# Turns of keys and outputs placed elsewhere, and a half slot in rounded passes, in a linear-attention and mixture-of-experts kernel

## The chip, the cores and the metric

One core of a Trainium2 chip. The time is that of one execution on the device, in microseconds (us). TensorE multiplies matrices, VectorE, ScalarE and GpSimd work on elements, and SyncE issues most of the DMAs.

## The reference

The first part is a linear attention with a decaying state, for 4 x 8 heads of 48 dimensions and 768 tokens:

```python
for t in range(S):
    state = alpha[:, :, t, :, None] * state + einsum('bhd,bhe->bhde', k[:, :, t], v[:, :, t])
    y[:, :, t] = einsum('bhd,bhde->bhe', q[:, :, t], state)
```

Its output, 3072 tokens of 384 numbers, goes through a mixture of 8 experts. Logits are `x @ w_gate` plus a bias by modality, each token goes to the expert of its largest logit, and the result is the softmax weight of that expert times `relu(x @ w1[e]) @ w2[e]`, with 1024 hidden numbers. Everything is in 32-bit floats.

## The kernel before, in words

**Attention.** A loop runs over steps `s` of 12 chunks (two batches of six chunks; a chunk is 128 tokens of two sequences, 16 heads, in two halves `z`). The steps are pipelined by hand: while VectorE scans the decays of a later chunk (`back`, `forth`) and GpSimd and VectorE scale keys and queries with them, TensorE works on chunk `s - 1`, and the output of chunk `s - 2` goes out. In step `s` TensorE does, in this order: `scores(s - 1, z)`, products of scaled keys and queries for both halves; `keys(s - 1)`, the transposes ("turns") of the scaled keys; `rows(s - 2)`, the turns of the outputs back to one row per token; `logits_turned(s - 2)`, the gate's logits; `from_state(s - 1)`, the products with the state; `add_logits(s - 2)`, from step 7 on, which sums ("folds") the logits over the heads' groups by products with a small table; `states(s - 1)`, the new state; `from_values(s - 1)`, masked scores times values. ScalarE copies each result out of PSUM (`scT` scores, `knat` keys, `xs` rows, `lts` logits, `yt` outputs) and passes over the decays once per chunk as a guard against extreme values (`junk`, `amin`). GpSimd masks the scores (`causal`).

Five PSUM banks `b0` to `b4` are handed out in turn (`next_bank`, line 119): a bank that comes up again must have been read before it is written. Scores take two, one per group of heads; key turns one per half; rows two; logits one; `from_state` two, which hold the outputs until `outputs` copies them at the start of the next step. Small products of the routing take one as well.

**Routing.** The tokens' experts are found in groups while the loop runs, and two early slots of 256 tokens are made up from the first chunks. In step 10 `count_early(0)` counts tokens per expert, and in step 11 `early_places(0)` (line 648) multiplies tables (`OL`, `OHE`) that VectorE makes from that count, to get the tokens of slot 0.

**Experts.** 12 slots of 256 tokens of one expert, then one half slot of 128. A product in full 32-bit precision is carried out as two passes; the slots use rounded operands (`F32R`), where a number is split into a high and a low part and a product takes three rounded passes. `layer1` (line 1197) runs `block` four times: six pairs of products, one of the high weights with high and low inputs side by side (512 columns), and one of the low weights with the high inputs (256 columns). ScalarE copies the low half out (`low`), VectorE adds (`hs`), ScalarE applies the relu and rounds (`hH`), VectorE makes the low part (`hL`), and both split two eighths of the second layer's weights (`w2H`, `w2L`). `layer2` (line 1213) then runs 24 products of 384 columns for each 128 tokens. The splits of the next slot's first-layer weights (`w1H`, `w1L`) stand inside `layer2`. `half` (line 1245) works otherwise: its first layer is in full precision, 24 products of 128 columns on unsplit weights.

**Order.** `Ordered` keeps every engine's instructions in the program's order until `order.clear()` (line 1322); `half(NS0)` comes after that, so that the planner may mix its instructions with those of slot 11. The routing for tokens that don't fit the 13 slots (`tail`) is not executed with these inputs.

Of the kernel before, what the change touches and what calls it, by code (L numbers as in the profile page):

```python
# [21 lines left out]
P = 128  # L22
# [12 lines left out]
T = 256  # L35
# [40 lines left out]
def attention_moe(ctx: ExitStack, tc: tile.TileContext, q, k, v, alpha, at_, kt_, qt_, vt_, mid, wg, wgp_, mb, w1, w2, out):  # L76
# [46 lines left out]
    def bank(*shape):  # L123
        return ps.tile([P, *shape], F32, name=next_bank())
# [241 lines left out]
                vec.tensor_copy(S1, kv)  # L366
            st[s, "S"] = S1

    def from_values(s):
        yk, vt = st[s, "yp"], VT[s % NV]  # L370
        for z in range(2):
            for j in range(NP):
                for x in range(2):
                    g = x ^ z
                    h = DM * z + D * head(z, j, g)
                    pe.matmul(
                        yof(yk, z, x, j),
                        vt[:, h : h + 64],
                        st[s, "s", z][:, g, j],
                        start=new(s, z, x),  # L380
                        stop=(j == NP - 1),
                    )
# [563 lines left out]
    for s in range(PS):  # L946
        if 0 < s and s + 1 < PS:
            load(s + 1, "kqv")
        if 0 <= s - 2:
            outputs(s - 2)  # L950
        late, by = [], vec
        if s == 0:
            warm(14)
            begin(0)
            for z in ZS:
                back(0, z)
                scaled_keys(0, z, pool)
                totals(0, z)
                forth(0, z)
                scaled_queries(0, z, pool if z == Z0 else vec)  # L960
        elif s == 1:
            begin(1)
            scores(0, 0)
            for z in range(2):
                turn_keys(0, z)
                if z == 0:
                    warm(2)
            back(1, Z0)
            scaled_keys(1, Z0, pool)
            scores(0, 1)  # L970
            totals(1, Z0)
            forth(1, Z0)
            scaled_queries(1, Z0, pool)
            back(1, Z1)
            scaled_keys(1, Z1, pool)
            totals(1, Z1)
            forth(1, Z1)
            scaled_queries(1, Z1)
        else:
            if (s - 1, "S") not in st:  # L980
                state(s - 1)
            decayed(s - 1)
            run(s, "state")
            for z in range(2):
                scores(s - 1, z)
            run(s, "masks")
            todo = scans(s)
            if len(todo) > 1:
                late = todo.pop()
            if s >= 4:  # L990
                by = pool
            for f in todo:
                do(f)
            run(s, "counts")
        if 1 < s:
            keys(s - 1)
        if 0 <= s - 2:
            rows(s - 2)
        if 0 <= 2 * (s - 3) < TURNED:
            turn_logits(s - 3)  # L1000
        if 0 <= s - 2:
            logits_turned(s - 2)
        run(s, "small")
        if 0 <= 2 * (s - 3) < TURNED:
            sum_logits(s - 3)
        run(s, "middle")
        do(late[:-1])
        if 0 <= s - 1:
            from_state(s - 1)
        if 0 <= s - 1 and (s - 1) % NC == 0:  # L1010
            states(s - 1)
        if TURNED <= 2 * (s - 2):
            add_logits(s - 2)
        if 0 <= s - 1 and (s - 1) % NC:
            states(s - 1)
        run(s, "sums")
        for f, *x in late[-1:]:
            f(*x, by)
        if 0 <= s - 1:
            from_values(s - 1)  # L1020
        run(s, "end")
        for c in range(s - (s < 5), s + 1 - (s < 4)):
            if 0 <= c < PS:
                guard(c)
        if 0 <= s - 2:
            store(s - 2)
        for c in range(s + 2 + (s > 4), s + 3 + (s > 3)):
            if c < PS:
                load(c, "a")
        if s == 0:  # L1030
            sp.dma_start(wgp, wgp_)
        if s == 1:
            sp.dma_start(mi.rearrange("p t w -> p (t w)"), mid.bitcast(I32))
            sp.dma_start(mbb, mb.unsqueeze(0).broadcast_to([P, NM, E]))
        if s == 2:
            sp.dma_start(xd[MID : MID + 1], of[0:1])
            sp.dma_start(gd[MID : MID + 1], of[0:1, 0:1])
# [135 lines left out]
    XL.append(XB[1][:, :, 1])  # L1173
    ms = {}

    def block(i, w1):
        wH, wL = w1
        hs = mp.tile([P, 2, T], F32, name="hs")
        low = mp.tile([P, 2, T], F32, name="low")
        for z in range(2):  # L1180
            hp = bank(2, T)
            fs = slice(z * P, (z + 1) * P)
            for d in range(ND):
                pe.matmul(hp, wH[:, d, fs], XB[i % 2][:, d], start=(d == 0), stop=False)
                pe.matmul(hp[:, 1], wL[:, d, fs], XH[i % 2][:, d], start=False, stop=(d == ND - 1))
            act.copy(low[:, z], hp[:, 1])
            vec.tensor_tensor(hs[:, z], hp[:, 0], low[:, z], op=ALU.add)
        return hs

    def second_input(hs):  # L1190
        hH = mp.tile([P, 2, T], F32R, name="hH", bufs=5)
        act.activation(hH, hs, AF.Relu)
        hL = mp3.tile([P, 2, T], F32R, name="hL", bufs=5)
        vec.scalar_tensor_tensor(hL, hs, 0.0, hH.bitcast(F32), op0=ALU.max, op1=ALU.subtract)
        return hH, hL

    def layer1(i, w1s):
        W2 = WR[i % 2][1]
        h, w2s = [], []
        for j in range(4):  # L1200
            hs = block(i, w1s[j])
            w2s.append(split("w2", W2[:, 2 * j : 2 * j + 2]))
            h.append(second_input(hs))
        ms[i] = h, w2s

    def scaled_out(i, u, op):
# [3 lines left out]
        if order and u == 0 and i in (NS0 // 2, NS0 - 1):  # L1210
            pool.drain()

    def layer2(i, ahead=()):
        h, w2s = ms[i]
        w1s = []
        for u in range(2):
            us = slice(u * P, (u + 1) * P)
            op = py.tile([P, 512], F32, name=f"y{u}")[:, :DM]
            for f in range(NF):
# [17 lines left out]

    def slot(i, w1s=None):
        layer1(i, w1s or [f() for f in w1_parts(i)])
        if i + 1 < NS and i < NS0:  # L1240
            prep(i + 1)
        refill(i + 2)
        return layer2(i, w1_parts(i + 1) if order and i + 1 < NS0 else ())

    def half(i):

        W1, W2 = WR[i % 2]
        g = gg[i % NX]
        hs, w2s = [], []
        w2s += [split("w2", W2[:, 2 * z : 2 * z + 2]) for z in (0, 1)]  # L1250
        for j in range(2):
            hp = bank(4, P)
            for z in range(4):
                fs = slice((4 * j + z) * P, (4 * j + z + 1) * P)
                for d in range(ND):
                    pe.matmul(hp[:, z], W1[:, d, fs], xf[:, d, :P], start=(d == 0), stop=(d == ND - 1))
            hH = mp.tile([P, 4, P], F32R, name="hH", bufs=5)
            relu = act.activation(hH, hp, AF.Relu)
            hL = mp3.tile([P, 4, P], F32R, name="hL", bufs=5)
            vec.scalar_tensor_tensor(hL, hp, 0.0, hH.bitcast(F32), op0=ALU.max, op1=ALU.subtract)  # L1260
            hs.append((hH, hL))
            if j == 0:
                with tc.issue_after(relu.ins):
                    w2s += [split("w2", W2[:, 2 * z : 2 * z + 2]) for z in (2, 3)]
        op = py.tile([P, 512], F32, name="y0")[:, :DM]
        for f in range(NF):
            (hH, hL), (wH, wL) = hs[f // 4], w2s[f // 2]
            pe.matmul(op, hH[:, f % 4], wH[:, f % 2], start=(f == 0), stop=False)
            pe.matmul(op, hH[:, f % 4], wL[:, f % 2], start=False, stop=False)
            pe.matmul(op, hL[:, f % 4], wH[:, f % 2], start=False, stop=(f == NF - 1))  # L1270
        os = mp3.tile([P, DM], F32, name="os", bufs=4)
        act.activation(os, op, AF.Copy, scale=g[:, 0:1])
        put(i, 0, os)

    def ahead_of(i):
        if i < NS:
# [2 lines left out]
    def tail(i):  # L1279
        if i < NS:  # L1280
            with tc.If(ns > i):
                if i > NS0:
                    gather(i)
                    gather_gates(i)
                    prep(i)
                with tc.If(nfl > i) as full:
                    ahead_of(i + 1)
                    act.copy(XH[i % 2], xf)
                    vec.tensor_tensor(XL[i % 2], xf, XH[i % 2].bitcast(F32), op=ALU.subtract)
                    slot(i)  # L1290
                with full.Else():
                    ahead_of(i + 1)
                    half(i)
                tail(i + 1)
# [24 lines left out]
    weights(2, 0, (1,))  # L1319
    for i in range(1, NS0):  # L1320
        w1s = slot(i, w1s)
    order.clear()
    half(NS0)

    anything = nc.values_load(more[0:1, 0:1], min_val=0, max_val=4 * P)  # L1325
    with tc.If(anything > 0):
# [85 lines left out]
```

## Time and profile before

| | |
|---|---|
| median of 3 runs | 343.76 us (342.46 to 344.66) |
| profiled execution | 343.79 us, span 342.1 us |
| TensorE products | 330.8 us busy, 97% of the span |
| TensorE weight loads | 300.7 us, 88% |
| VectorE | 265.7 us, 78% |
| ScalarE | 229.5 us, 67% |
| GpSimd | 170.8 us, 50% |

The profiled execution lies on the median. Busy shares are means over the span. A product is shown from its issue to its modelled end; products overlap, so the distance from start to start tells what one costs in a stream. TensorE's granted clock is full over the whole of its work.

### The profile page before, as it was taken

The page shows a single profiled execution, that of the slowest core. Times are in us where ns is not written, and L with a number is a line of the kernel's source. Part 1 is how long each engine was busy: PE and PEld are TensorE (multiplying, and loading weights), DVE is VectorE, ACT ScalarE, POOL GpSimd, SP SyncE. Part 2 cuts the span into 40 slices and gives each one's busy share as a digit, 9 for nine tenths or more (in the row PEclk, how much of TensorE's full clock was granted, in tenths as well). Part 3 has the DMA queues.
Part 4 walks back from the last instruction along what each step waited for, and adds up shares of the span by engine and source line. Part 5 has one row for each costly group of instructions (what it writes and reads, how often), then busy time and mean ns, then how long its engine had stood idle before and what let it go on. Part 6 is the DMA issues. An engine that isn't in the chain of part 4 may idle for free. (4 is left out here: it accounts for less than half of the span.)

```text
span 342.1 us, 8364 instructions
## 1 busy us (share of the span) xinstructions
PE 330.8 (97%) x3162; PEld 300.7 (88%) x3162; DVE 265.7 (78%) x487; ACT 229.5 (67%) x454; POOL 170.8 (50%) x185
## 2 busy tenths in 40 slices
PE   6899999999999999999999999999999999999991
PEld 6788888888888977999999999999898989898990
DVE  6999999999985876959696868686878777787430
ACT  1767978767686516858585868686868676767430
POOL 7778799788767047554252524251444252411021
PEclk9999999999999999999999999999999999999998
DMA  7998899986185956997867676667586767660010
GB/s 231 398 398 297 288 321 321 327 297 248 44 283 148 375 215 229 372 383 253 258 217 231 210 248 225 227 223 219 164 295 219 223 209 246 205 208 23 1 50 32
DMA packets 39799, 80.07 MB, mean 234 GB/s; under 512 B 3867, under 2 KB 20404, under 8 KB 39748
## 3 DMA queue, kind: packets, MB, share of 16 engines
q1 hardware_dynamic: 35652, 69.38, 58.8%
q0 software_dynamic: 4096, 10.05, 8.9%
q8 instruction: 27, 0.44, 0.5%
q14 instruction: 24, 0.20, 0.2%
HBM read 69.77 MB, written 9.65 MB: 232 GB/s over the span
## 5 line engine op out<-in xcount | busy, mean ns | idle before, releaser
L66 PE MATMUL b<-xHL,w1H 128*128 128x512 f32 (+1 forms) x312 | 102.6, 378 | 0.0
L66 POOL DMA_INDIRECT out_dram<-os,idx x25 | 27.2, 1087 | 110.4 <-ACT os L66 70.8
L66 PE MATMUL b<-xHL,w1L 128*128 128x256 f32 x288 | 80.6, 280 | 0.0
L66 PEld LDWEIGHTS b<-xHL,w1H 128*128 128x128 f32 x312 | 57.4, 188 | 11.3 <-issue 0.4
L66 PE MATMUL y<-w2H,hH 128*128 128x384 f32 x184 | 62.6, 340 | 0.0
L66 PE MATMUL y<-w2H,hL 128*128 128x384 f32 x184 | 61.7, 335 | 0.0
L66 PE MATMUL y<-w2L,hH 128*128 128x384 f32 x184 | 61.6, 335 | 0.0
L66 DVE TENSOR_TENSOR hs<-b,low 128x256 f32<-128x256 f32 x88 | 33.9, 415 | 32.6 <-ACT low L66 32.6
L66 PEld LDWEIGHTS b<-xHL,w1L 128*128 128x128 f32 x288 | 54.2, 188 | 0.1
L66 DVE TENSOR_TENSOR w1L<-w1r,w1H 128x768 fp32r<-128x768 f32 x48 | 43.8, 951 | 6.6 <-ACT w1H L66 6.3
L66 DVE TENSOR_TENSOR w2L<-w2r,w2H 128x768 fp32r<-128x768 f32 x48 | 45.8, 958 | 3.4 <-ACT w2H L66 3.4
L66 ACT ACTIVATE os<-y,gg 128x384 f32<-128x384 f32 x25 | 14.6, 583 | 39.7 <-PE y L66 39.7
L66 ACT CAST w2H<-w2r 128x768 fp32r<-128x768 f32 x48 | 40.0, 841 | 0.0
L66 ACT COPY low<-b 128x256 f32<-128x256 f32 x88 | 30.1, 367 | 14.5 <-PE b L66 14.5
L66 POOL DMA_INDIRECT xg<-xd,idx x26 | 29.4, 1130 | 18.7 <-DVE idx L66 11.0
L66 ACT CAST w1H<-w1r 128x768 fp32r<-128x768 f32 x48 | 37.9, 839 | 0.8 <-ACT ls L66 0.8
L66 POOL DMA_INDIRECT gg<-gd,idx x26 | 28.7, 1103 | 18.7 <-issue 13.1
L66 PEld LDWEIGHTS y<-w2L,hH 128*128 128x128 f32 x184 | 34.6, 188 | 0.0
L66 PEld LDWEIGHTS y<-w2H,hH 128*128 128x128 f32 x184 | 34.6, 188 | 0.0
L66 PEld LDWEIGHTS y<-w2H,hL 128*128 128x128 f32 x184 | 34.5, 188 | 0.0
L66 ACT COPY scT<-b 128x512 f32<-128x512 f32 x48 | 24.8, 599 | 14.2 <-PE b L66 13.1
L66 POOL TENSOR_TENSOR kh<-kt,G 128x512 f32<-128x512 f32 x24 | 30.5, 1278 | 6.3 <-DVE G L66 5.7
(180 smaller groups left out, 593.7 us busy)
## 6 DMA issues: line engine op xcount, KB each, us to landing
w1r<-in_w_dram SPq DMA_DIRECT2D x26, 768.0 KB, 5.4
w2r<-in_w_dram SPq DMA_DIRECT2D x26, 768.0 KB, 5.8
X<-in_turned_alpha_dram SPq DMA_DIRECT2D x10, 516.5 KB, 5.3
kt<-in_turned_k_dram SPq DMA_DIRECT2D x10, 512.0 KB, 5.5
qt<-in_turned_q_dram SPq DMA_DIRECT2D x10, 512.0 KB, 6.6
vt<-in_paired_v_dram SPq DMA_DIRECT2D x12, 384.0 KB, 6.2
xd<-xs SPq DMA_DIRECT2D x12, 384.0 KB, 4.9
kt<-in_turned_k_dram SPq DMA_DIRECT2D x4, 256.0 KB, 2.8
```

The lines of the kernel that those rows point to most:

```text
L66: ins = f(*a, **kw)
```

## The change

Three things. In the first steps, the first half of the key turns of chunk 1 moves from step 2 into step 1, between the halves of `from_values(0)`, and `rows(0)` moves between the halves of `scores(1)`. From step 7 on (`folded`) `rows(s - 2)` moves from before the logits to behind `from_state`, ahead of the fold. The half slot uses `layer1` and `layer2` of the other slots with 128 columns (`n`) and one group of tokens (`us=1`), with its inputs turned in `half_inputs`; its first-layer weights are split within slot 11, and it stays in the program's order.

```diff
@@ -366,9 +366,9 @@
                 vec.tensor_copy(S1, kv)
             st[s, "S"] = S1
 
-    def from_values(s):
+    def from_values(s, zs=(0, 1)):
         yk, vt = st[s, "yp"], VT[s % NV]
-        for z in range(2):
+        for z in zs:
             for j in range(NP):
                 for x in range(2):
                     g = x ^ z
@@ -981,8 +981,10 @@
                 state(s - 1)
             decayed(s - 1)
             run(s, "state")
-            for z in range(2):
-                scores(s - 1, z)
+            scores(s - 1, 0)
+            if s == 2:
+                rows(0)
+            scores(s - 1, 1)
             run(s, "masks")
             todo = scans(s)
             if len(todo) > 1:
@@ -992,9 +994,12 @@
             for f in todo:
                 do(f)
             run(s, "counts")
-        if 1 < s:
+        if s == 2:
+            turn_keys(1, 1)
+        elif s > 2:
             keys(s - 1)
-        if 0 <= s - 2:
+        folded = TURNED <= 2 * (s - 2)
+        if s > 2 and not folded:
             rows(s - 2)
         if 0 <= 2 * (s - 3) < TURNED:
             turn_logits(s - 3)
@@ -1007,16 +1012,22 @@
         do(late[:-1])
         if 0 <= s - 1:
             from_state(s - 1)
+        if folded:
+            rows(s - 2)
         if 0 <= s - 1 and (s - 1) % NC == 0:
             states(s - 1)
-        if TURNED <= 2 * (s - 2):
+        if folded:
             add_logits(s - 2)
         if 0 <= s - 1 and (s - 1) % NC:
             states(s - 1)
         run(s, "sums")
         for f, *x in late[-1:]:
             f(*x, by)
-        if 0 <= s - 1:
+        if s == 1:
+            from_values(0, (0,))
+            turn_keys(1, 0)
+            from_values(0, (1,))
+        elif s > 1:
             from_values(s - 1)
         run(s, "end")
         for c in range(s - (s < 5), s + 1 - (s < 4)):
@@ -1173,34 +1184,34 @@
     XL.append(XB[1][:, :, 1])
     ms = {}
 
-    def block(i, w1):
+    def block(i, w1, n):
         wH, wL = w1
-        hs = mp.tile([P, 2, T], F32, name="hs")
-        low = mp.tile([P, 2, T], F32, name="low")
+        hs = mp.tile([P, 2, T], F32, name="hs")[:, :, :n]
+        low = mp.tile([P, 2, T], F32, name="low")[:, :, :n]
         for z in range(2):
-            hp = bank(2, T)
+            hp = bank(2, n)
             fs = slice(z * P, (z + 1) * P)
             for d in range(ND):
-                pe.matmul(hp, wH[:, d, fs], XB[i % 2][:, d], start=(d == 0), stop=False)
-                pe.matmul(hp[:, 1], wL[:, d, fs], XH[i % 2][:, d], start=False, stop=(d == ND - 1))
+                pe.matmul(hp, wH[:, d, fs], XB[i % 2][:, d, :, :n], start=(d == 0), stop=False)
+                pe.matmul(hp[:, 1], wL[:, d, fs], XH[i % 2][:, d, :n], start=False, stop=(d == ND - 1))
             act.copy(low[:, z], hp[:, 1])
             vec.tensor_tensor(hs[:, z], hp[:, 0], low[:, z], op=ALU.add)
         return hs
 
-    def second_input(hs):
-        hH = mp.tile([P, 2, T], F32R, name="hH", bufs=5)
+    def second_input(hs, n):
+        hH = mp.tile([P, 2, T], F32R, name="hH", bufs=5)[:, :, :n]
         act.activation(hH, hs, AF.Relu)
-        hL = mp3.tile([P, 2, T], F32R, name="hL", bufs=5)
+        hL = mp3.tile([P, 2, T], F32R, name="hL", bufs=5)[:, :, :n]
         vec.scalar_tensor_tensor(hL, hs, 0.0, hH.bitcast(F32), op0=ALU.max, op1=ALU.subtract)
         return hH, hL
 
-    def layer1(i, w1s):
+    def layer1(i, w1s, n=T):
         W2 = WR[i % 2][1]
         h, w2s = [], []
         for j in range(4):
-            hs = block(i, w1s[j])
+            hs = block(i, w1s[j], n)
             w2s.append(split("w2", W2[:, 2 * j : 2 * j + 2]))
-            h.append(second_input(hs))
+            h.append(second_input(hs, n))
         ms[i] = h, w2s
 
     def scaled_out(i, u, op):
@@ -1210,10 +1221,10 @@
         if order and u == 0 and i in (NS0 // 2, NS0 - 1):
             pool.drain()
 
-    def layer2(i, ahead=()):
+    def layer2(i, ahead=(), us=2):
         h, w2s = ms[i]
         w1s = []
-        for u in range(2):
+        for u in range(us):
             us = slice(u * P, (u + 1) * P)
             op = py.tile([P, 512], F32, name=f"y{u}")[:, :DM]
             for f in range(NF):
@@ -1237,40 +1248,29 @@
 
     def slot(i, w1s=None):
         layer1(i, w1s or [f() for f in w1_parts(i)])
-        if i + 1 < NS and i < NS0:
+        if i + 1 < NS0:
             prep(i + 1)
+        elif i + 1 == NS0:
+            half_inputs(NS0)
         refill(i + 2)
-        return layer2(i, w1_parts(i + 1) if order and i + 1 < NS0 else ())
-
-    def half(i):
...
-            hp = bank(4, P)
-            for z in range(4):
-                fs = slice((4 * j + z) * P, (4 * j + z + 1) * P)
-                for d in range(ND):
-                    pe.matmul(hp[:, z], W1[:, d, fs], xf[:, d, :P], start=(d == 0), stop=(d == ND - 1))
...
+        return layer2(i, w1_parts(i + 1) if order and i < NS0 else ())
+
+    def half_inputs(i):
+        x = xg[i % NX]
+        xp = ps.tile([P, 4, P], F32, name="kv")[:, :ND]
+        for d in range(ND):
+            pe.transpose(xp[:, d], x[:, 0, d * P : (d + 1) * P], ident)
+        split_inputs(i, xp, P)
+
+    def split_inputs(i, x, n=T):
+        act.copy(XH[i % 2][:, :, :n], x)
+        vec.tensor_tensor(XL[i % 2][:, :, :n], x, XH[i % 2][:, :, :n].bitcast(F32), op=ALU.subtract)
+
+    def half(i, w1s=None):
+        if not w1s:
+            split_inputs(i, xf[:, :, :P], P)
+        layer1(i, w1s or [f() for f in w1_parts(i)], P)
+        layer2(i, us=1)
 
     def ahead_of(i):
         if i < NS:
...
@@ -1319,8 +1318,8 @@
     weights(2, 0, (1,))
     for i in range(1, NS0):
         w1s = slot(i, w1s)
+    half(NS0, w1s)
     order.clear()
-    half(NS0)
 
     anything = nc.values_load(more[0:1, 0:1], min_val=0, max_val=4 * P)
     with tc.If(anything > 0):
```

## Rows read from the trace of the kernel before

**Rows 1.** Windows: length, then each engine's busy us (instructions), granted clock, DMA share, GB/s.

```profile
17.00:25.60 8.60, 8.60 (x159) 7.56 (x159) 8.32 (x11) 5.90 (x14) 6.59 (x6) 1.00 1.03 397
...
34.20:68.00 33.80, 33.80 (x572) 29.61 (x569) 31.84 (x45) 27.91 (x61) 29.55 (x28) 1.00 0.91 313
```

**Rows 2.** Timeline of TensorE, first steps: start, us, engine, operation, idle before.

```profile
13.90 1.09 PE L66 MATMUL b<-scT,vt 128*64 128x128 f32 x16 [0.34 <-POOL scT L66]
15.06 1.16 PE L66 MATMUL b<-qh,kh 48*128 48x128 f32 x16
16.84 1.16 PE L66 MATMUL b<-qh,kh 48*128 48x128 f32 x16 [0.62 <-DVE qh L66]
...
18.87 1.04 PE L66 MATMUL b<-ident,yt 128*128 128x128 f32 x8
19.83 0.64 PE L66 MATMUL b<-yt,wgp 128*32 128x256 f32 x8
```

**Rows 3.** Timeline of ScalarE, first steps.

```profile
12.57 1.17 ACT L66 ACTIVATE junk<-X,bhi 128x1033 bf16<-128x1033 uint32 x1
```

**Rows 4.** Timeline, 34 to 66 us: GpSimd, then TensorE, then VectorE.

```profile
42.08 1.18 POOL L66 TENSOR_TENSOR kh<-kt,G 128x512 f32<-128x512 f32 x1 [0.66 <-DVE G L66]
...
52.94 2.59 POOL L66 TENSOR_SCALAR_AFFINE_SELECT scT<-scT 128x1024 f32<-128x1024 f32 x2
...
54.80 1.97 PE L66 MATMUL b<-scT,vt 128*64 128x128 f32 x32
56.70 2.06 PE L66 MATMUL b<-qh,kh 48*128 48x128 f32 x32
...
35.30 1.57 DVE L66 TENSOR_TENSOR qh<-qt,Fw 128x512 f32<-128x512 f32 x1
...
46.53 0.69 DVE L66 TENSOR_TENSOR qh<-qt,Fw 128x512 f32<-128x512 f32 x1
```

**Rows 5.** Timeline, steps 10 and 11: ScalarE, then VectorE.

```profile
91.64 0.59 ACT L66 COPY yt<-b 128x512 f32<-128x512 f32 x1 [2.09 <-PE b L66]
92.51 0.59 ACT L66 COPY yt<-b 128x512 f32<-128x512 f32 x1 [0.29 <-PE b L66]
...
96.28 0.19 DVE L66 TENSOR_TENSOR OHE<-OHE,room 128x32 f16<-128x32 f16 x1
```

**Rows 6.** Timeline of TensorE, steps 10 and 11.

```profile
92.39 2.06 PE L66 MATMUL b<-qh,kh 48*128 48x128 f32 x32
...
96.84 0.55 PE L66 MATMUL b<-OHE,OL 128*128 128x2 f16 x16
```

**Rows 7.** Timeline of slot 11 and the half slot: TensorE, then VectorE.

```profile
320.08 3.06 PE L66 MATMUL b<-xf,w1r 128*128 128x128 f32 x26
322.90 0.42 PE L66 MATMUL y<-w2H,hL 128*128 128x384 f32 x1
...
327.84 2.62 PE L66 MATMUL b<-xf,w1r 128*128 128x128 f32 x22
330.21 0.42 PE L66 MATMUL y<-w2H,hH 128*128 128x384 f32 x1
...
313.99 0.68 DVE L66 SCALAR_TENSOR_TENSOR hL<-hs,hH 128x512 fp32r<-128x512 f32 x1
...
315.26 0.95 DVE L66 TENSOR_TENSOR w2L<-w2r,w2H 128x768 fp32r<-128x768 f32 x1
316.12 0.68 DVE L66 SCALAR_TENSOR_TENSOR hL<-hs,hH 128x512 fp32r<-128x512 f32 x1
```

**Rows 8.** Timeline of TensorE: narrow passes and rounded passes of 256 columns.

```profile
79.64 0.61 PE L66 MATMUL kv<-fold,lts 128*128 128x8 f32 x4
80.18 1.14 PE L66 MATMUL kv<-vt,knat 128*64 128x48 f32 x32
...
110.14 0.28 PE L66 MATMUL b<-xHL,w1L 128*128 128x256 f32 x1
110.26 0.28 PE L66 MATMUL b<-xHL,w1H 128*128 128x256 f32 x1
```

More of the change, by code (lines that the diff above doesn't have):

```diff
@@ L1239, in slot @@
         layer1(i, w1s or [f() for f in w1_parts(i)])
-        if i + 1 < NS and i < NS0:
+        if i + 1 < NS0:
             prep(i + 1)
+        elif i + 1 == NS0:
+            half_inputs(NS0)
         refill(i + 2)
-        return layer2(i, w1_parts(i + 1) if order and i + 1 < NS0 else ())
-    def half(i):
[L1247 to L1251, printed above, removed]
-            hp = bank(4, P)
-            for z in range(4):
-                fs = slice((4 * j + z) * P, (4 * j + z + 1) * P)
-                for d in range(ND):
-                    pe.matmul(hp[:, z], W1[:, d, fs], xf[:, d, :P], start=(d == 0), stop=(d == ND - 1))
[L1257 to L1273, printed above, removed]
@@ L1284, in tail @@
                     gather_gates(i)
-                    prep(i)
+                prep(i)
                 with tc.If(nfl > i) as full:
                     ahead_of(i + 1)
-                    act.copy(XH[i % 2], xf)
-                    vec.tensor_tensor(XL[i % 2], xf, XH[i % 2].bitcast(F32), op=ALU.subtract)
+                    split_inputs(i, xf)
                     slot(i)
```

## The prediction

> **What bounds the kernel now.** I read the page's engine shares first, then windows, then the order of single instructions. The shares put TensorE far ahead, but they are a mean over stages. Between 34 and 68 us TensorE has no idle time at all, and VectorE has 31.84 of 33.80 us in the same window [rows 1]: two engines run neck and neck, so a microsecond saved on TensorE is worth one only while VectorE, or what hangs on it, is not the next to be late. The pauses that the change wants to fill are in the first steps. The values' second half starts at 13.90 after 0.34 us of waiting for GpSimd's mask, and the second scores of chunk 1 at 16.84 after 0.62 us of waiting for VectorE's scaled queries [rows 2]. In the windows behind them TensorE's busy time fills the window (8.60 of 8.60 us from 17 us on [rows 1]).
>
> The profiled execution took 343.79 us (span 342.1, and 1.7 around it), 0.03 from the median of 343.76, so sums against it hold for the median too.
>
> **Turns in the first steps.** Nothing is added or taken away: four key turns go between the two halves of the values of chunk 0, the eight output turns of chunk 0 go between the two halves of the scores of chunk 1, and four key turns stay. Eight turns take 0.96 us (18.87 to 19.83) [rows 2], 0.12 each. No DMA is issued by them.
> - Key turns: the values' first half is over by 13.56 (13.90 less 0.34). With 0.48 us of turns and a change of operand shape (some 0.1 us) the second half starts near 14.1 instead of 13.90. Such a half takes 0.95 us elsewhere (half of 1.90, 54.80 to 56.70 [rows 4]), while here the scores follow 1.16 us after it, at 15.06 [rows 2]: they wait for GpSimd's queries and stay where they are. The cost is nothing, and those queries cover it; without that cover it would be 0.2 us.
> - On ScalarE the copy of the turned keys (0.6 us) now stands ahead of the guard's pass of 1.17 us, which began at 12.57 [rows 3]. The guard therefore starts at about 14.7, and the two output copies behind it, 0.55 us each, end at about 17.0. The output turns wait for them: they end near 17.5, and the second scores start near 17.6 instead of 16.84. What is then left is 1.1 us of scores, 0.48 us of turns and a shape change, so the logits start near 19.25 instead of 19.83 [rows 2]. That is a gain of 0.6 us (bounds: 0.96, both pauses, and nothing). The load of chunk 3's decays waits for the guard and is issued 2 us later; the queue is busy then (1.03 of 16 engines' time from 17 us on [rows 1]), so it only loses its place in a backlog.
> - How much of it lasts? VectorE has no slack to give, and GpSimd follows it: the scaled keys at 42.08 wait for VectorE's scan, and the masks of chunk 5 follow back to back and end at 55.53 (52.94 and 2.59). TensorE starts the half that needs the second mask at the middle of its 1.90 us of values, 55.75 [rows 4]. It can come earlier by 0.2 us at most, 0.15 with the semaphore. From there on I count a gain of **0.15 us**, not 0.6.
>
> **Outputs turned beside the fold (steps 7 to 11).** The eight turns go from before the logits to behind the products with the state. As many instructions, and as many shape changes except one more in step 7 (about 0.1 us). Two new waits:
> - The five PSUM banks go round in turn. With two banks taken by the output turns after the products with the state, the next scores' second bank is one that still holds an output. In four steps the copy is through in time. In step 10 the expert count takes a fifth bank, so that step 11's first scores need both outputs' banks: the second copy ends at 93.10 (92.51 and 0.59) [rows 5], while those scores start at 92.39 [rows 6] and meet that bank at their second product, about 92.6. A wait of 0.5 us; behind it stand the keys' turns and all that follows.
> - In step 11 the places of the early slot (96.84) need VectorE's table, ready at 96.47 (96.28 and 0.19) [rows 5], so they had 0.37 us to spare [rows 6]. Before, the output turns filled the time until then. Now TensorE comes to it 0.96 us of work earlier, waits until about 96.5, and still has the turns to do: late by 0.96 - 0.37 + 0.05 = 0.64. The bank wait lies inside this one: whatever TensorE gained or lost before 96.5 is swallowed, the 0.15 us too.
>
> I take **+0.6 us**. Bounds: +0.4, if VectorE comes to this table earlier by more than it did, so that only the bank wait less the 0.15 stays; +1.5, since VectorE's scaled queries took 0.69 at one place and 1.57 at another [rows 4], as they met GpSimd's work or not, and one such change in its chain moves the table. The logits' copy comes earlier on ScalarE and the rows' copy later; it has 2.09 us idle ahead of the first output copy [rows 5], which covers both. The stores leave about 1 us later; the gathers that read those rows come later still, so I cost it at nothing.
>
> **The half slot.** Before, its first layer was 48 full-precision passes of 128 columns, which ran as filler in slot 11's second layer: 320.08 to 322.90 and 327.84 to 330.21 [rows 7]: 2.82 + 2.37 = 5.19 us. TensorE had no gap there. After, it is 24 rounded pairs, one product of 256 columns and one of 128.
> - The 256 columns: 0.12 us (110.14 to 110.26) [rows 8].
> - A rounded pass of 128 columns is not in the trace. Below: half of 0.12, 0.06. Above: two full-precision passes, 2 x 0.108 = 0.217. I take 0.112, by the fold's passes: they have 8 columns, and four of them still hold TensorE from 79.64 to 80.18 [rows 8], 0.135 each with a shape change, so columns don't set that time; the load of 128 columns of weights does, and the narrow pass has the same load.
> - 24 x (0.12 + 0.112) = 5.57 us, against 5.19: +0.38. Ends: 4.3 and 8.1.
> - Six turns of inputs become three: -0.36.
> - The second layer, 24 passes, is unchanged. Its weights' splits were partly ahead of the half and now stand in program order inside each block, on ScalarE and VectorE. VectorE takes 2.13 us a block at 256 tokens (313.99 to 316.12 [rows 7]), of which the weights' split keeps its 0.95 and the rest about halves: 1.55. The first part of the layer is out 0.7 us after its start, 1.2 with its copy, so the fourth block's result is ready 1.2 + 4 x 1.55 = 7.4 us after the start; TensorE asks for it at 5.57 + 3 x 1.04 + 0.35 = 9.0. No wait (upper bound, at 2.13 a block: 9.7, so 0.7). The new splits of the first layer's weights, four on each engine, lie beside slot 11's second layer (8.3 us), as in every slot before.
>
> Sum of the tail: **0.0 us** (-1.2 to +2.5). Total: 343.79 + 0.6 + 0.0 = **344.4 us**.
>
> **Rivals.**
> - A: the narrow pass runs with its weight load hidden, at 0.06 us: 4.3 us instead of 5.57, so 344.4 - 1.25 = 343.2. For: in the wide pairs no load shows. Against: the fold. Chance 0.13. The Trainium skill (TensorE: Matmul & The Clock Gate, Back-to-back issue gap) states about 81 ns a product for a stream of loads and products at 128 columns; by that the layer would be 24 x 0.201 = 4.8 us and the time 343.7, between this and the forecast. No row here shows it.
> - B: the moved turns pay after all, because GpSimd's chain shifts with the earlier scores, and the table of step 11 comes early: 343.79 - 0.6 = 343.2. Against it is that VectorE has nothing idle from 34 to 68 us but 2 us in 34. Chance 0.12.
> - C, the slow side: the narrow rounded pass is no cheaper than a full-precision product, 0.217 us: 344.4 + 2.5 = 346.9. For: no rounded product under 256 columns stands in the trace, and the kernel has used wide ones throughout. Against: nothing in the rows makes a pass dearer for being narrow. It decides from 0.13 us a pass upward; at 0.24 the kernel is slower by 1%. Chance 0.17.
> - D: the planner lays the moved turns where they were, or the waits fall in gaps that the trace doesn't show: 343.8. Chance 0.10.
>
> **How the numbers follow.** The forecast has 0.48: 344.4, with 343.9 to 345.3 as its own range. A measurement of this kernel can tell about 1%, 3.4 us, from no change. Even both pauses and the cheapest narrow pass together, 0.96 + 1.2, do not reach that, so faster by over 1% has 0.03; slower has the upper part of C, with a long VectorE chain beside it, 0.09; the rest is 0.88. The range from 342.6 to 346.6 takes A, B and D with their ends, and leaves out most of C.
>
> **What would show it.** Right: the two pauses at 13.6 and 16.2 are gone or moved, the logits of chunk 0 start near 19.3, and the values of chunk 5 still start their second half within 0.1 us after the mask. In step 11 TensorE waits near 92.6 for the output copy or near 96 for the table, and from there all is 0.6 us later. The half's pairs start 0.23 us apart. Wrong: pairs 0.18 or 0.34 apart (A, C), a wait between the half's layers, or TensorE passing 100 us earlier than before (B).

## The result and the profile after

The changed kernel took 345.65 us (median of 13 runs, 344.54 to 347.06), the kernel before 343.77 us beside it (13 runs, 342.30 to 345.67): a ratio of 1.0057, 95% interval 1.0034 to 1.0081, so **1.9 us longer**, under one per cent and yet outside the scatter. The medians of the kernel before differ from one session to another by up to 0.9 us; parts are therefore compared by their ratios, each to the runs of before in its own session.

The page of the changed kernel, its engine shares:

```profile
span 345.3 us, 8391 instructions
PE 332.8 (96%) x3159; PEld 301.2 (87%) x3159; DVE 273.9 (79%) x502; ACT 235.0 (68%) x467; POOL 172.3 (50%) x185
```

This execution took 347.01 us, 1.36 above the median. The second half of its first scores started 1.28 us later than in the trace of before (11.73, there 10.45), since one input came later and VectorE's scaled queries of the second unit (the second half of chunk 0) took 1.55 us instead of 0.69. Nothing that the change touches comes ahead of that point, so I take differences from one point to the next. Timeline of TensorE in the first steps (start, duration in us, operation, idle before and what ended it):

```profile
14.78 0.66 PE L66 MATMUL b<-ident,kh 128*128 128x128 f32 x4
15.36 1.09 PE L66 MATMUL b<-scT,vt 128*64 128x128 f32 x16
16.39 1.16 PE L66 MATMUL b<-qh,kh 48*128 48x128 f32 x16
17.89 1.14 PE L66 MATMUL b<-ident,yt 128*128 128x128 f32 x8 [0.34 <-ACT yt L66]
18.97 1.16 PE L66 MATMUL b<-qh,kh 48*128 48x128 f32 x16
20.64 0.64 PE L66 MATMUL b<-yt,wgp 128*32 128x256 f32 x8
```

The waits of 0.34 and 0.62 us [rows 2] are gone, one of 0.34 for the output copy has come. The logits stand 0.81 us later than before instead of 1.28: a gain of 0.47 us. It does not last: at the scores of step 7 (58.53, before 56.70) TensorE is 1.83 us late, 1.02 more than at those logits. In step 7 the trace shows three waits that before had not:

```profile
57.50 1.09 PE L66 MATMUL b<-scT,vt 128*64 128x128 f32 x16 [0.17 <-POOL scT L66]
58.53 2.06 PE L66 MATMUL b<-qh,kh 48*128 48x128 f32 x32
...
62.86 0.66 PE L66 MATMUL b<-ident,yt 128*128 128x128 f32 x4 [0.47 <-ACT knat L66]
64.26 0.66 PE L66 MATMUL b<-ident,yt 128*128 128x128 f32 x4 [0.74 <-DVE room L66]
...
68.35 2.05 PE L66 MATMUL b<-qh,kh 48*128 48x128 f32 x32
```

The values of chunk 5, which before ran through in one piece [rows 4], wait for the mask. The output turns of chunk 5 then wait twice for a PSUM bank: 0.47 us for ScalarE's copy of the keys, and 0.74 us for VectorE's sum of the logits of chunk 4. VectorE comes to that sum late, behind its scan and scaled queries:

```profile
62.25 1.54 DVE L66 TENSOR_TENSOR qh<-qt,Fw 128x512 f32<-128x512 f32 x1
63.97 0.23 DVE L66 TENSOR_REDUCE room<-b 128x16 f32<-128x64 f32 x1
```

From the scores at 58.53 (1.83 later than before) to the next scores at 68.35 (3.47 later) the changed kernel loses **1.64 us**. In step 11 it loses 0.71 (its scores are 3.34 us late, the next step's 4.05), in the wait for an output's bank ahead of the third product:

```profile
95.73 0.49 PE L66 MATMUL b<-qh,kh 48*128 48x128 f32 x2
96.48 2.05 PE L66 MATMUL b<-qh,kh 48*128 48x128 f32 x30 [0.27 <-ACT yt L66]
```

The half slot runs without a gap between its pairs and its layers; its first layer begins and ends so:

```profile
328.74 0.28 PE L66 MATMUL b<-xHL,w1H 128*128 128x256 f32 x1
...
334.00 0.34 PE L66 MATMUL b<-xHL,w1H 128*128 128x256 f32 x1
334.18 0.22 PE L66 MATMUL b<-xHL,w1L 128*128 128x128 f32 x1
334.24 0.39 PE L66 MATMUL y<-w2H,hH 128*128 128x384 f32 x1
```

24 pairs in 334.24 - 328.74 = 5.50 us, 0.229 each. From the last logits to the last product TensorE takes 222.68 us (115.60 to 338.28) against 222.84 before (111.45 to 334.29): 0.16 us less. The last product, before and then after:

```profile
334.29 0.34 PE L66 MATMUL y<-w2H,hL 128*128 128x384 f32 x1
```

```profile
338.28 0.34 PE L66 MATMUL y<-w2H,hL 128*128 128x384 f32 x1
```

From its end to the end of the span (342.1 and 345.3) it is 7.44 us before and 6.67 after, 0.77 less. So, apart from the late start, TensorE gains 0.47 us, loses 1.02, 1.64 and 0.71, and 0.16 and 0.77 are saved at the end: 2.0 us, about what the medians show.

### The profile page after: what moved, and what is told of

Same layout as the page of the kernel before. It is cut to its first block, busy times and chain, and to the rows that moved or that the text cites. A ratio compares the mean times of both kernels' runs of the same rounds, so it can differ in the third digit from the quotient of the medians.

```text
span 345.3 us, 8391 instructions
## 1 busy us (share of the span) xinstructions
PE 332.8 (96%) x3159; PEld 301.2 (87%) x3159; DVE 273.9 (79%) x502; ACT 235.0 (68%) x467; POOL 172.3 (50%) x185
## 5 line engine op out<-in xcount | busy, mean ns | idle before, releaser
L66 PE MATMUL b<-xHL,w1H 128*128 128x512 f32 (+1 forms) x336 | 108.2, 375 | 0.0
L66 PE MATMUL b<-xHL,w1L 128*128 128x256 f32 (+1 forms) x312 | 85.9, 276 | 0.0
L66 PEld LDWEIGHTS b<-xHL,w1H 128*128 128x128 f32 x336 | 61.9, 188 | 11.3 <-issue 0.4
L66 DVE TENSOR_TENSOR hs<-b,low 128x256 f32<-128x256 f32 (+1 forms) x96 | 35.9, 404 | 35.0 <-ACT low L66 35.0
L66 PEld LDWEIGHTS b<-xHL,w1L 128*128 128x128 f32 x312 | 58.8, 188 | 0.1
L66 DVE TENSOR_TENSOR w1L<-w1r,w1H 128x768 fp32r<-128x768 f32 x52 | 47.8, 957 | 7.6 <-ACT w1H L66 7.2
L66 DVE TENSOR_TENSOR w2L<-w2r,w2H 128x768 fp32r<-128x768 f32 x48 | 45.9, 956 | 3.8 <-ACT w2H L66 3.8
L66 ACT COPY low<-b 128x256 f32<-128x256 f32 (+1 forms) x96 | 31.9, 359 | 15.0 <-PE b L66 14.9
L66 ACT CAST w1H<-w1r 128x768 fp32r<-128x768 f32 x52 | 41.0, 838 | 0.0
L66 POOL DMA_INDIRECT xg<-xd,idx x26 | 32.0, 1231 | 16.0 <-DVE idx L66 8.0
L66 ACT ACTIVATE hH<-hs 128x512 fp32r<-128x512 f32 (+1 forms) x48 | 29.5, 615 | 8.5 <-DVE hs L66 8.3
```

The lines of the kernel that those rows point to most:

```text
L66: ins = f(*a, **kw)
```

## Experiments

All were timed in five rounds against the kernel before. In the short diffs "-" is the line of before, or of the kernel named.

**The parts one by one.** First the moves of the first steps alone:

```
+            scores(s - 1, 0)
+            if s == 2:
+                rows(0)
+            scores(s - 1, 1)
...
+            from_values(0, (0,))
+            turn_keys(1, 0)
+            from_values(0, (1,))
```

> Only the moves in the first steps (key turns of chunk 1 between the halves of the values of chunk 0, output turns of chunk 0 between the halves of the scores of chunk 1). Theory (VectorE and the masks that follow it set the pace): chunk 0's logits start 0.5 us earlier against the first scores, and nothing of it is left behind the masks of chunk 5, whose half starts 0.05 us after the mask; 343.6 to 343.8 us. Rival (TensorE is the bound, the moves pay): about 0.5 us less than before, 343.2. Second rival (the moves are what made the changed kernel slower): 345 or more.

Measured: 344.67 us (343.26 to 346.18), ratio 1.0037 (1.0013 to 1.0061). Neither nothing nor a gain: the moves that fill pauses make the kernel 1.3 us slower.

Then the output turns alone, moved behind the products with the state from step 7 on:

```
+        folded = TURNED <= 2 * (s - 2)
-        if 0 <= s - 2:
+        if 0 <= s - 2 and not folded:
...
+        if folded:
+            rows(s - 2)
```

> Only the output turns moved behind the products with the state, from step 7 on. Theory (waits for PSUM banks): in step 7 the turns wait about 1.4 us, for the copy of the keys and for VectorE's sum of the turned logits, and a shape change adds 0.2; in step 11 the scores' second bank waits 0.5 to 0.6 us; together 345.7 to 346.2 us, all of the loss of the changed kernel. Rival (the loss comes from the first steps or from the half slot): 343.5 to 344.2.

Measured: 345.96 us (seven runs), ratio 1.0079 (1.0051 to 1.0108), 2.7 us slower. Its trace has the two bank waits of step 7 again, 0.47 us for ScalarE's copy of the keys and 0.66 for VectorE's sum.

Third, the half slot alone in rounded passes (`block`, `second_input`, `layer1` and `layer2` with a width, no `half`):

> Only the half slot in rounded passes. Theory: pairs 0.23 us apart, no wait between its layers, the last product 0.1 to 0.2 us earlier than before against slot 11's second layer; 343.5 to 343.8 us. Rival (the half's added splits and order cost): 344.5 or more.

Measured: 342.74 us (342.22 to 342.95), ratio 0.9978 (0.9958 to 0.9997): 0.75 us faster. Its trace shows the 0.16 us above, and more behind the last product: 6.37 us to the end of the span, against 7.44 before. The three traces without the rounded half slot take 7.44 to 7.62 us there, the eleven with it 6.29 to 7.42; which of its edits shortens that stretch, no run tells. Its 12 runs lie within 0.73 us, those of before within 2.8; why, no run tells. The three parts by themselves come to 1.3 + 2.7 - 0.75 = 3.2 us, together they cost 1.9.

Fourth, the changed kernel with step 7's output turns in their old place:

```
-        folded = TURNED <= 2 * (s - 2)
+        folded = 8 <= s
```

> The changed kernel, but in step 7 the output turns stand where they were. Theory (bank waits): the wait of step 7 is gone, that of step 11 stays; 1.4 to 1.7 us less than the changed kernel, 344.0 to 344.4. Rival (step 7's wait only shows lateness that comes from VectorE anyway, and would show elsewhere): 345.2 to 345.7.

Measured: 343.92 us, ratio 1.0019 (1.0000 to 1.0038). Against 1.0057 that is 0.38%, **1.3 us for step 7** alone, the largest single piece of the loss. The trace agrees: from the scores of step 7 to the next it takes 8.18 us (57.04 to 65.22), as before (56.70 to 64.88), where the changed kernel took 9.82.

**Step 11: the bank, or the table?** The fourth kernel, and two banks passed over ahead of the scores of step 11:

```
+            if s == 11:
+                next_bank(), next_bank()
```

> The change with step 7's output turns in their old place (as the run that came to 343.92 us) and, besides, two PSUM banks passed over ahead of the scores of step 11, so that the scores no longer ask for a bank that still holds an output. Theory (the bank wait of step 11, 0.55 us in the trace of the changed kernel, stands on the path): 343.3 to 343.5 us, the second product of those scores starts 0.12 us after the first, and TensorE is 0.5 us earlier at 100 us. Rival (the table for the places of the early slot, or VectorE ahead of it, is late next and swallows it): 343.8 to 344.0 us with a new wait ahead of the places of the early slot.

Measured: 344.42 us, ratio 1.0023 (1.0002 to 1.0044), no gain over 1.0019. Timelines of TensorE in step 11, first with the bank wait (the fourth kernel), then without it:

```profile
92.60 0.49 PE L66 MATMUL b<-qh,kh 48*128 48x128 f32 x2
93.35 2.05 PE L66 MATMUL b<-qh,kh 48*128 48x128 f32 x30 [0.27 <-ACT yt L66]
95.33 1.09 PE L66 MATMUL b<-ident,kh 128*128 128x128 f32 x8
...
96.93 0.55 PE L66 MATMUL b<-OHE,OL 128*128 128x2 f16 x16
```

```profile
92.60 2.06 PE L66 MATMUL b<-qh,kh 48*128 48x128 f32 x32
94.58 1.09 PE L66 MATMUL b<-ident,kh 128*128 128x128 f32 x8
...
96.74 0.55 PE L66 MATMUL b<-OHE,OL 128*128 128x2 f16 x16 [0.49 <-DVE OHE L66]
```

The scores run through: the key turns start 1.98 us after the first score instead of 2.73, so the bank cost 0.75 us, and the row's 0.27 us of idle time shows only a part of it. Three groups later TensorE waits 0.49 us for VectorE's table, and 0.19 us are left (96.93 to 96.74). A part of that is this run's own: an operation of VectorE ahead of the table (`left` from `taken`, at 95.46 in both traces) took 0.65 us, where with the bank wait it took 0.17. With 0.17 us there TensorE would have come to the table just as it was ready (some 96.2). The medians side with the rival, no gain, but one trace does not show how often the table is the one that is late.

The same move from step 8 on, beside the half slot alone:

> The kernel before with the half slot in rounded passes and the output turns moved behind the products with the state from step 8 on, the first steps untouched. Theory (step 11's bank wait of 0.55 us is all that this move costs, nothing is gained): 343.2 to 343.4 us. Rival (the move from step 8 on brings TensorE's turns behind something that it would else wait for, as the sum of the single runs suggests): 342.2 to 342.6 us, faster than the half slot alone.

Measured: 343.54 us, ratio 1.0007 (0.9990 to 1.0025), against 0.9978 for the half slot alone: 1.0 us more, where its trace shows 0.65 us. Beside the half slot alone the move costs and brings nothing.

**Which of the first moves costs?** The half slot with the key turns moved, and the half slot with the output turns moved:

> The kernel before with the half slot in rounded passes and only the key turns of the first steps moved; the output turns stay where they were. Theory (the copy of the turned keys goes ahead of the guard on ScalarE, GpSimd's masks and scaled keys shift and meet VectorE's scaled queries, which take longer, so that the mask of chunk 5 is later and TensorE waits for it): 343.2 to 343.8 us against 342.7 for the half slot alone, the mask of chunk 5 ends 45.9 us or more after the scaled queries of the second unit. Rival (the turns in the pauses are free): 342.5 to 342.8 us.

> The kernel before with the half slot in rounded passes and only the output turns of chunk 0 moved between the scores; the key turns stay where they were. Theory (the guard keeps its place on ScalarE, so that less of VectorE's chain shifts): 342.6 to 343.1 us. Rival (it is the second scores, behind turns that wait for ScalarE, which delay GpSimd's masks and so VectorE): 343.3 to 344.0 us, and the mask of chunk 5 as late as with both moves.

Measured: key turns 342.79 us, ratio 0.9980 (0.9960 to 1.0000), as the half slot alone (0.9978): free, my theory fell. Output turns 343.44 us, ratio 0.9998 (0.9978 to 1.0017): 0.7 us more, the rival; the two kernels, timed side by side, differ by 0.65. In the second trace TensorE comes 0.4 us earlier to the logits of chunk 0 than with the half slot alone, and at the scores of step 7 it is 1.16 us behind (57.52, there 56.36), after two waits that the half slot alone does not have:

```profile
46.05 1.10 PE L66 MATMUL b<-qh,UB 64*64 64x128 f32 x32 [0.31 <-POOL UB L66]
...
56.50 1.09 PE L66 MATMUL b<-scT,vt 128*64 128x128 f32 x16 [0.48 <-POOL scT L66]
```

GpSimd is late for both, and it is late because it waits for VectorE, 2.25 us for a scan where before it waited 0.66 [rows 4]:

```profile
42.52 1.19 POOL L66 TENSOR_TENSOR kh<-kt,G 128x512 f32<-128x512 f32 x1 [2.25 <-DVE G L66]
```

VectorE in turn is late because its scaled queries meet GpSimd in another order. The kernel before near 27.5 us, VectorE, then GpSimd (two masks under one row):

```profile
27.37 0.99 DVE L66 TENSOR_TENSOR qh<-qt,Fw 128x512 f32<-128x512 f32 x1
...
26.72 2.59 POOL L66 TENSOR_SCALAR_AFFINE_SELECT scT<-scT 128x1024 f32<-128x1024 f32 x2 [1.08 <-ACT scT L66]
```

The first steps' moves alone, the same stretch:

```profile
27.57 1.44 DVE L66 TENSOR_TENSOR qh<-qt,Fw 128x512 f32<-128x512 f32 x1
31.94 0.96 DVE L66 TENSOR_TENSOR qh<-qt,Fw 128x512 f32<-128x512 f32 x1
...
26.33 2.14 POOL L66 TENSOR_SCALAR_AFFINE_SELECT scT<-scT 128x1024 f32<-128x1024 f32 x2 [0.49 <-ACT scT L66]
```

Before, the masks take 2.59 us and the queries 0.99; with TensorE ahead the masks start 0.4 us earlier, take 2.14, and the queries 1.44. Together they take 3.58 us both times: who starts first keeps its time, the other pays. It is the second of the two masks that changes places with the queries (27.37 and 27.57). GpSimd's timeline from 27.9 us before, and from 27.5 us with the moves, shows it by itself:

```profile
27.78 1.54 POOL L66 TENSOR_SCALAR_AFFINE_SELECT scT<-scT 128x1024 f32<-128x1024 f32 x1
```

```profile
27.38 1.09 POOL L66 TENSOR_SCALAR_AFFINE_SELECT scT<-scT 128x1024 f32<-128x1024 f32 x1
```

The fourteen traces bear this out: in 207 of VectorE's 210 scaled queries, the time above 0.69 us is, to 0.01 us, the overlap with an operation of GpSimd (mask, scaled keys or queries, product with the state) that had begun earlier, less 0.14 us, and nothing where they overlap by less. In the three others a mask began 0.03 us behind the queries, and these waited for it all the same, 0.98 us. Here GpSimd has idle time to pay from (before, it is busy 7.17 of the 8.60 us from 25.60 on, VectorE 8.17).

**Both moves of the first steps with the half slot**, as the base for two tests of that:

> Both moves of the first steps and the half slot in rounded passes, the output turns of the later steps where they were. Theory (the half slot gives 0.7 us, the moves of the first steps cost what they cost alone): 343.8 to 344.2 us; the mask of chunk 5 ends 45.9 us or more after the scaled queries of the second unit, and TensorE waits for it. Rival (the two parts depend on each other, since the move of the outputs from step 8 on cost 1.0 us beside the half slot alone but nothing beside these moves): 343.0 us or less, or 344.8 us or more.

Measured: 344.60 us, ratio 1.0011 (0.9992 to 1.0030), 1.1 us over the half slot alone by the ratios (0.9978), as the single parts say. (With the output turns moved from step 8 on besides, the fourth kernel, it was 1.0019: not told apart, so that move's 1.0 us does not show here.) Its profiled run, though, fell otherwise. The gain of the first steps is gone already behind scaled queries of 1.50 us in step 2, but no more than that: the mask of chunk 5 ends only 45.5 us after the second unit's queries, where 45.9 or more was expected, TensorE does not wait for it, and at the scores of step 12 it is level with the half slot alone (101.45, there 101.40). It loses 1.22 us from there to the first slot (110.88, there 109.61), and 0.85 us more lie behind the last product (7.22 against 6.37). ScalarE, then TensorE:

```profile
102.83 0.58 ACT L66 COPY yt<-b 128x512 f32<-128x512 f32 x1 [1.01 <-PE b L66]
...
110.88 0.39 PE L66 MATMUL b<-xHL,w1H 128*128 128x256 f32 x1 [0.52 <-ACT yt L66]
```

The product that this copy waits for ended at 101.52; with the half slot alone the copy followed 0.05 us behind it. Near 101 and 110 us all four kernels timed together last (this one and the three below) have such copies late, by 0.55 to 1.4 us; in the ten other traces, also of kernels with the same moves, none is later than 0.4. Why, no run tells. So one profile shows one of the ways that a run can take, and this one does not show the 1.1 us to come from VectorE and GpSimd.

**More work, later.** The same kernel, and GpSimd masks three quarters of chunk 2's first scores twice:

```
+        if s == 2 and z == 0:
+            part = sc[:, :, :, :96]
+            pool.affine_select(part, part, [[0, 2], [0, NP], [1, 96]], ALU.is_ge, 0.0, base=0, channel_multiplier=-1)
```

> As the run with both moves of the first steps and the half slot, and GpSimd masks three quarters of chunk 2's first scores twice (the second pass changes no value): some 0.8 us more work on GpSimd, so that its masks of chunk 2 begin after VectorE's scaled queries, as in the kernel before, and not ahead of them. Theory (who of VectorE and GpSimd starts first keeps its speed, the other is held up; with the turns moved GpSimd came first): VectorE's scaled queries near 27.5 us take 1.0 us instead of 1.44 and those near 32 us 0.7 instead of 0.96, the mask of chunk 5 ends 0.5 us earlier, and the kernel with MORE work is 0.4 to 0.7 us faster than the one without. Rival (the added work delays GpSimd's chain, and the length of VectorE's operations has another cause): as long or up to 0.8 us longer.

Measured: 343.31 us, ratio 0.9972 (0.9954 to 0.9991) against 1.0011 (0.9992 to 1.0030): with 0.88 us more work on GpSimd **1.3 us faster**, more than expected. VectorE, then GpSimd:

```profile
27.41 1.32 DVE L66 TENSOR_TENSOR qh<-qt,Fw 128x512 f32<-128x512 f32 x1
31.66 0.86 DVE L66 TENSOR_TENSOR qh<-qt,Fw 128x512 f32<-128x512 f32 x1
35.63 0.69 DVE L66 TENSOR_TENSOR qh<-qt,Fw 128x512 f32<-128x512 f32 x1
...
26.15 3.54 POOL L66 TENSOR_SCALAR_AFFINE_SELECT scT<-scT 128x768 f32<-128x768 f32 x3 [0.47 <-ACT scT L66]
```

The sign holds. Against the trace of the first steps' moves alone the mechanism does too, at another place than the one I named: the queries near 27.4 fell only to 1.32, those near 31.7 to 0.86, while the third, 1.50 in the run of the moves alone, has 0.69. The mask of chunk 5 ends 44.8 us after the second unit's queries, against 45.9 there, and TensorE has none of the two waits. That this makes the 1.3 us is not shown: in the trace of the same kernel without the added mask TensorE reaches the scores of step 12 even earlier (101.45, here 101.59), and what it loses, it loses behind them.

**GpSimd's bias table out of the way** (0.58 to 1.02 us, moved to the end of step 6), and both edits together:

```
-    for m in range(NM + 1):
+    for m in range(NM):
         at(3 + m, "masks", bias_table, m)
+    at(6, "end", bias_table, NM)
```

> As the run with both moves of the first steps and the half slot, and GpSimd's table of the biases for the third group, 0.58 to 1.02 us of GpSimd between the masks of chunk 4 and the scaled keys of chunk 5, moved behind the latter to the end of step 6. Theory (TensorE waits for GpSimd's mask of chunk 5, and VectorE's chain alone is late by less): 0.3 to 0.6 us under the run without this, the mask of chunk 5 earlier by 0.5 us. Rival (the mask waits for VectorE's scaled queries, GpSimd would only idle earlier): no difference within 0.2 us.

> The last two edits together, on both moves of the first steps and the half slot: the table of the biases later and chunk 2's first mask partly done twice. Theory (both waits of TensorE, for GpSimd's product with the state near 48 us and for the mask of chunk 5 near 57 us, go, so that the 0.47 us gained in the first steps stays): 342.2 to 342.7 us, under the half slot alone. Rival (the next wait on VectorE takes it back): 342.8 to 343.5 us.

Measured: 344.03 us, ratio 1.0004 (0.9985 to 1.0023), 0.57 us less by the medians but not told apart from 1.0011; and 343.80 us, ratio 0.9998 (0.9979 to 1.0017), against 0.9972 without the later table. Relieving GpSimd's chain gains nothing that can be told from the scatter, and both together are no better than the doubled mask: a miss. Beside the later table the doubled mask also brings nothing that can be told apart (343.80 against 344.03), so its gain stands in one of two comparisons. In the first of the two traces the mask of chunk 5 still ends 45.8 us after the second unit's queries, since other pieces of GpSimd and VectorE now meet. In the second the wait of 0.34 us ahead of the first slot has come in, as above. The best times are the half slot alone, with or without the key turns (0.9978, 0.9980), and the doubled mask (0.9972); no run separates these three.

## Why the prediction came out as it did

The forecast of 344.4 us was 1.25 us short of the median. By its steps:

- **Key turns: right.** They are free (0.9980 against 0.9978).
- **Output turns of the first step: the gain was right, what becomes of it was wrong.** 0.6 us was forecast at the logits, 0.47 measured. "From there on I count a gain of 0.15 us" held VectorE's chain fixed while TensorE, and so GpSimd, came earlier. In fact GpSimd's masks moved ahead of VectorE's queries, VectorE paid, and the gain became a loss of 0.7 us (output turns alone) to 1.1 and 1.3 (both moves, with and without the half slot; the trace of the 1.1 does not show this cause). The rows had it, 0.69 and 1.57 for one operation [rows 4], and I used it only as the upper end of another term. The range of this one had no loss in it.
- **Step 7: the mis-sized term.** "One more in step 7 (about 0.1 us)", a shape change, was all that the forecast had there: step 7 measured 1.64 us in the trace and 1.3 between the kernels. I followed the five banks to step 11 and not through step 7, where the turned logits and the keys hold two of them, and where the one reader, VectorE's sum, stands behind its scan and queries. Before, the output turns stood ahead of the logits' turn and never asked for its bank.
- **Step 11: near in size, by the other wait.** The 0.6 us were worked out from the table (0.96 - 0.37 + 0.05), with the bank's wait inside them. The table's wait did not show in the changed kernel, as TensorE came late to it (100.06, ready at 98.18). What it lost there, 0.71 us, is the wait for the second output's bank, forecast at 0.5 and measured at 0.75; that the sum fits is luck. With the bank free and the turns of step 7 in their old place, a wait of 0.49 us for it did appear, though that run's table was itself late.
- **The half slot: right in TensorE, with nothing for what comes behind it.** 0.232 us a pair forecast, 0.229 measured, no wait between the layers (VectorE's blocks 1.6 us apart, 1.55 forecast), the tail to the last product -0.16 us against 0.0. Rivals A (0.18 a pair) and C (0.34) are out, and so are the 0.201 between them. In medians it is worth 0.75 us (0.1 to 1.4): besides the 0.16 its traces show a shorter stretch behind the last product, by 0.77 us in the changed kernel, and the sum had no term for that.
- **Luck in the total.** That gain met part of what the first steps and step 7 were short of; without it the forecast would have missed by about 2 us.
- **Rivals B and D fell**: no table came early, and the turns did move.

What stays open: why moves that cost 0.6 us in the trace (first steps alone, from the second unit's queries to the last logits) cost 1.3 in medians. Part of it is the trace of before, taken from a run of 343.79 us, 0.57 above the median of the session in which these moves were timed. Their runs scatter by 2.9 us and one profile each shows one order of meetings. Nor does a run show why both moves beside the half slot cost 1.1 us, why ScalarE's copies came late in one session, what shortens the stretch behind the last product, or how often the table of step 11 is late.

## What to carry to other kernels

Filling a pause on the busiest engine moves every engine that it feeds: before counting the gain, look which operations of two neighbours now start in another order, above all where one of them has no idle time. When work is moved past other users of a small ring of buffers, walk the ring through every step that differs, not only through the one that looks tight, and price a buffer by when its last reader comes to it. Ahead of a point that another engine sets, look for the wait that comes next before taking one away.

## What the runs showed of the hardware

- VectorE's product of 128x512 took 0.69 us undisturbed and up to 1.69 beside GpSimd; of the two engines the one that began first kept its time (masks 2.14 and queries 1.44, or 2.59 and 0.99: 3.58 both times), and the other took longer by their overlap less 0.14 us (207 of 210 queries; in three a mask that began 0.03 us later went first).
- A rounded product of 128 columns in a pair with one of 256 brings the pair to 0.229 us, where a product of 256 columns takes 0.12 in a wide pair [rows 8]: halving the columns saved next to nothing.
- Adding 0.88 us of GpSimd's work went with a time shorter by 1.3 us in one comparison (343.31 against 344.60) and by nothing that can be told apart in another (343.80 against 344.03).
- With the rounded half slot the stretch behind the last product took 6.29 to 7.42 us in eleven traces, without it 7.44 to 7.62 in three.
